# Attention by blocks of 512 queries, with a block's output product, norm and FFN issued between the next block's scores and the FFN weight parts kept in DRAM

## The chip, the core and the metric

One NeuronCore of one Trainium2 chip runs the whole program. The metric is the device time of one execution in microseconds (us). A core has a matrix engine (PE, with its own weight loads, PEld), a vector engine (DVE), a scalar engine (ACT), a general engine (POOL) and a queue engine (SP) that here issues most DMAs. Each engine takes its instructions in the order in which they were put down; engines wait for one another by semaphores.

## The reference, cut to what matters

One transformer block on 2048 rows of 576 numbers in f32, with 32 heads of 18 numbers each and a hidden width of 4608:

```
x = A_x                                            # 1 x 2048 x 576
h = x + softmax(q k^T / sqrt(18)) v @ wo           # q, k, v = layernorm(x) @ wqkv, 32 heads
g, u = layernorm(h) @ w_gate, layernorm(h) @ w_up  # 576 x 4608 each
out = h + (gelu_tanh(g) * u) @ w_down              # 4608 x 576
```

## The kernel before

**Numbers.** Every large product is made of f16 pieces: a matrix is kept as a high part and a low part, and `products` lists the 14 pairs of 128-row pieces that `accumulate` multiplies into one PSUM bank (three pairs for each of four full row chunks, two for the 64-row rest). A chunk of 512 output columns is thus 14 matmuls 512 wide, a half row block (288 columns) 14 matmuls 288 wide. The down product uses 12 matmuls 288 wide per chunk (four hidden tiles, three pairs).

**Stages.** First the rows are normed, split and transposed by DMA into `X`, and q, k (`qk_tile`) and v (`v_rows`) are made; q and k go to DRAM as `qk_hi` and `qk_lo`, v stays in SBUF. Then come 32 attention stages: eight groups of four heads (outer loop), and for each group four blocks of 512 queries (inner loop). A stage has 16 key tiles with two head pairs each: 32 slots. A slot has

- two score matmuls of one head pair (`scores_pair`, line 461; each uses 56 rows of the array, the two lie in different halves) into one of two PSUM pairs, and one ACT exponential over both (line 463), 128 x 1024 numbers;
- two matmuls (line 420) and two DVE maxima (line 423) of a stage that lies 56 slots ahead (`maxima`), through three PSUM banks `bank0` to `bank2`; the maxima become two rows of the next stages' q operand (`max_finish`);
- in every second slot the four f32 matmuls of `weigh` (line 467) that multiply the exponentials with v; each fills 32 of the 128 partitions of `acc`, and the trace shows each as two.

After a stage `out_block` transposes, divides and stores its result in f16 parts. Remaining q, k and v products run in between at the start (`other_products`). With the last group, `wo_block` of a finished query block fills in. When all attention is done the FFN runs: for 9 chunks of 512 hidden columns and 4 row blocks, `gate_up` makes 4 x 2 chunks of 14 matmuls, and `down` of the chunk before 8 chunks of 12. The FFN weights of a chunk are loaded from the inputs once, and split on ACT and DVE beside the chunk before.

**Order.** Inside `tc.manual_schedule` the PE order is the order of the code; the other engines' order is set by the framework's scheduler. The FFN lies behind that region.

Of the kernel before, what the change touches and what calls it, by code (L numbers as in the profile page):

```python
# [8 lines left out]

F16 = mybir.dt.float16  # L10
# [6 lines left out]
P = 128  # L17
# [8 lines left out]
MSC = 4096.0  # L26


@with_exitstack
def tile_block(  # L30
# [16 lines left out]

    nc = tc.nc
# [5 lines left out]
    TB = min(512, S)  # L54
    NB = S // TB
    TPB = TB // P
    FT = 4
    FC = FT * P
    NCH = DF // FC
    QK = 2 * D  # L60
    NG = H // 4
    R1 = 3 * DH

# [6 lines left out]
    pairs2 = [ps.tile([P, 2, 512], F32, name=f"pair{i}") for i in range(2)]  # L70
    singles = [ps.tile([P, 512], F32, name=f"bank{i}") for i in range(4)]
# [5 lines left out]
    pair_ring = ring(pairs2)  # L77
    single_ring = ring([p[:, i] for i in range(2) for p in pairs2])
    m_ring = ring(singles[:3])
    down_ring = ring(singles)  # L80


    nat = const.tile([P, NT, D], F32, name="nat")
    V = const.tile([P, 9936], F32, name="V")
    X = const.tile([P, 18432], F16, name="X")
    W = const.tile([P, 18048], F16, name="W")
    WK = const.tile([P, 2 * (NK + 1) * D], F32, name="WK")
    A = const.tile([P, 3 * 2048], F32, name="A")
# [25 lines left out]
    def exponents(views, name):  # L114

        n = len(views)
        k = views[0].shape[1]
        ac = small.tile([P, n, k], F32, tag=f"ac{n}", name=f"ac_{name}")
        am = small.tile([P, n], F32, tag=f"am{n}", name=f"am_{name}")
        for i, v in enumerate(views):  # L120
            for c in range(k):
                nc.vector.tensor_reduce(ac[:, i, c : c + 1], v[:, c], axis=AX.X, op=ALU.max,
                                        apply_absolute_value=True)
                yield
        nc.vector.tensor_reduce(am, ac, axis=AX.X, op=ALU.max)
        yield
        pt = next(m_ring)
        for i in range(n):
            nc.tensor.transpose(pt[0:1, i * P : (i + 1) * P], am[:, i : i + 1], id32)
        a1 = small.tile([1, n], F32, tag=f"a1{n}", name=f"a1_{name}")  # L130
        nc.vector.tensor_reduce(a1, pt[0:1, : n * P].rearrange("o (n p) -> o n p", n=n),
                                axis=AX.X, op=ALU.max)
        nc.vector.tensor_scalar_max(a1, a1, 2.0 ** -60)
        yield
        pb = next(m_ring)
        nc.tensor.matmul(pb[:, :n], ones[0:1], a1, start=True, stop=True)
        ab = small.tile([P, n], F32, tag=f"ab{n}", name=f"ab_{name}")
        nc.vector.tensor_copy(ab, pb[:, :n])
        e = small.tile([P, n], I32, tag=f"e_{name}", name=f"e_{name}")
        nc.vector.tensor_scalar(e, ab.bitcast(I32), 23, None, op0=ALU.logical_shift_right)  # L140
        yield
        return e

    def norm_exponent(v, name):

        q = small.tile([P, 2], F32, tag="nq", name=f"nq_{name}")
        j = view(A, 8 * 2 * 2 * D, (NK, D), F16)
        nc.scalar.activation(j, v[:, :NK], AF.Square, accum_out=q[:, 0:1])
        nc.scalar.activation(j[:, 0], v[:, NK], AF.Square, accum_out=q[:, 1:2])
        pb = next(m_ring)  # L150
        nc.tensor.matmul(pb[:, :2], ones, q, start=True, stop=True)
        a = small.tile([P, 1], F32, tag="na", name=f"na_{name}")
        nc.vector.tensor_reduce(a, pb[:, :2], axis=AX.X, op=ALU.add)
        nc.vector.tensor_scalar_max(a, a, 2.0 ** -110)
        e = small.tile([P, 1], I32, tag=f"e_{name}", name=f"e_{name}")
# [605 lines left out]
```

## Time and profile before

| | |
|---|---|
| median of three runs | 3018.15 us (3017.2 to 3020.59) |
| the profiled execution | 3017.52 us, of which its span (first to last instruction) is 3015.8 us |
| mean granted PE clock | 0.995 |
| DVE, ACT, POOL busy | 1993.3, 1454.6 and 62.9 us |
| DMA | 95.14 MB moved, mean 32 GB/s |
| first maxima, first scores, end of attention | about 95, 223 and 1693 us after the span's start |

Busy time of PE is modelled from matmuls that overlap; how much work PE really has is read from the start of one matmul to the start of the next. A line number in a row is that of the source line; many matmuls carry the line of the helper `accumulate` (267), so that the tiles' names tell them apart.

### The profile page before, as it was taken

The page shows a single profiled execution, that of the slowest core. Times are in us where ns is not written, and L with a number is a line of the kernel's source. Part 1 is how long each engine was busy: PE and PEld are TensorE (multiplying, and loading weights), DVE is VectorE, ACT ScalarE, POOL GpSimd, SP SyncE. Part 2 cuts the span into 40 slices and gives each one's busy share as a digit, 9 for nine tenths or more (in the row PEclk, how much of TensorE's full clock was granted, in tenths as well). Part 3 has the DMA queues.
Part 4 walks back from the last instruction along what each step waited for, and adds up shares of the span by engine and source line. Part 5 has one row for each costly group of instructions (what it writes and reads, how often), then busy time and mean ns, then how long its engine had stood idle before and what let it go on. Part 6 is the DMA issues. An engine that isn't in the chain of part 4 may idle for free.

```text
span 3015.8 us, 42951 instructions
## 1 busy us (share of the span) xinstructions
PE 2792.8 (93%) x17312; PEld 1154.9 (38%) x17312; DVE 1993.3 (66%) x3711; ACT 1454.6 (48%) x1716; POOL 62.9 (2%) x137
## 2 busy tenths in 40 slices
PE   6998888888888888888889999999999999999999
PEld 3531112212111211211123455555555555555555
DVE  7569999999999999999996653443435252524222
ACT  5227777777777777777757422121212121212111
POOL 0000000000000000000000000000000000000000
PEclk9999999999999999999999999999999999999999
DMA  8121000000100000000023420110101010100001
GB/s 222 49 87 32 1 25 1 25 1 1 25 1 25 1 24 2 1 24 5 29 48 87 100 67 7 45 33 19 51 1 52 1 51 1 51 1 1 1 16 48
DMA packets 105433, 95.14 MB, mean 32 GB/s; under 512 B 65872, under 2 KB 79312, under 8 KB 105232
## 3 DMA queue, kind: packets, MB, share of 16 engines
q1 hardware_dynamic: 100256, 83.81, 9.8%
q0 software_dynamic: 4976, 8.56, 1.1%
q8 instruction: 136, 2.23, 0.3%
q14 instruction: 65, 0.53, 0.1%
HBM read 63.70 MB, written 14.16 MB: 26 GB/s over the span
## 4 chain that ended last, share of the span: by engine, by line
PE 74%; DVE 18%; ACT 4%; issue 2%; DMA 2%; SPq 0%; DVEq 0%; ACTq 0%
PE pair L267 30%; PE bank L267 16%; DVE mx L423 15%; PE bank L467 14%; PE bank L420 9%; PE pair L461 4%; ACT WK L463 1%; ACT W L238 1%; ACT V L238 1%; PE bank L480 1%; DVE o L485 0%; ACT V L598 0%; DVE nat L491 0%; DMA A<-qk_hi 0%; DMA WK<-in_A_wqkv_dram 0%
## 5 line engine op out<-in xcount | busy, mean ns | idle before, releaser
L423 DVE TENSOR_REDUCE mx<-bank 128x1 f32<-128x512 f32 x2048 | 1283.2, 682 | 138.4 <-PE bank L420 137.4
L463 ACT ACTIVATE WK<-pair,p_ex_sc 128x1024 f32<-128x1024 f32 x1024 | 1088.0, 1112 | 335.1 <-PE pair L461 333.4
L467 PE MATMUL bank<-WK,V 128*32 128x512 f32 x4096 | 551.9, 610 | 0.1
L267 PE MATMUL pair<-X,V 128*128 128x512 f16 x2240 | 489.0, 379 | 3.1 <-ACT ga L613 3.1
L267 PE MATMUL pair<-X,W 128*128 128x512 f16 x2128 | 469.0, 379 | 1.5 <-ACT ga L613 1.5
L615 DVE SCALAR_TENSOR_TENSOR ga<-pair,p_hsc,ga 128x512 f32<-128x512 f32 x144 | 107.7, 748 | 502.4 <-PE pair L267 502.4
L420 PE MATMUL bank<-W 54*128 54x512 f16 x1024 | 291.5, 378 | 93.2 <-DVE mx L423 91.1
L267 PEld LDWEIGHTS <-WK 128*128 128x128 f16 x3456 | 338.2, 98 | 93.2
L420 PE MATMUL bank<-A 54*128 54x512 f16 x1024 | 283.0, 380 | 80.5 <-DVE mx L423 77.7
L613 ACT ACTIVATE ga<-pair,p_gsc 128x512 f32<-128x512 f32 x144 | 98.8, 686 | 490.2 <-PE pair L267 490.2
L267 PEld LDWEIGHTS <-W 128*128 128x128 f16 x2296 | 222.2, 98 | 273.1 <-issue 16.9
L267 PEld LDWEIGHTS <-V 128*128 128x128 f16 x2240 | 218.7, 98 | 261.6 <-issue 3.9
L616 ACT CAST WK<-ga 128x512 f16<-128x512 f32 x144 | 88.9, 618 | 442.9 <-DVE ga L615 442.9
L634 DVE SCALAR_TENSOR_TENSOR nat<-bank,p_dsc,nat 128x288 f32<-128x288 f32 x288 | 147.9, 515 | 194.9 <-PE bank L267 194.9
L467 PEld LDWEIGHTS bank<-WK,V 128*32 128x32 f32 x4096 | 81.3, 108 | 504.5 <-issue 469.0
L267 PE MATMUL bank<-V,WK 128*128 128x288 f16 x1920 | 239.0, 286 | 0.0
L461 PE MATMUL pair<-W 56*128 56x512 f16 x1024 | 199.1, 384 | 5.8 <-ACT WK L463 5.6
L461 PE MATMUL pair<-A 56*128 56x512 f16 x1024 | 199.9, 385 | 0.3 <-DVE qk L322 0.2
L267 PE MATMUL bank<-W,WK 128*128 128x288 f16 x1536 | 191.4, 286 | 0.0
L617 DVE TENSOR_TENSOR WK<-ga,WK 128x512 f16<-128x512 f32 x144 | 99.3, 690 | 76.3 <-ACT WK L616 76.1
L461 PEld LDWEIGHTS <-W 56*128 56x128 f16 x1024 | 50.2, 94 | 247.9 <-issue 221.0
L461 PEld LDWEIGHTS <-A 56*128 56x128 f16 x1024 | 50.5, 95 | 241.3 <-issue 211.0
(154 smaller groups left out, 1122.0 us busy)
## 6 DMA issues: line engine op xcount, KB each, us to landing
V<-in_B_w_down_dram SPq DMA_DIRECT2D x9, 1152.0 KB
A<-in_B_w_gate_dram SPq DMA_DIRECT2D x9, 1024.0 KB
A<-in_B_w_up_dram SPq DMA_DIRECT2D x9, 1024.0 KB
qk_hi<-qk SPq DMA_DIRECT2D x36, 128.0 KB
qk_lo<-qk SPq DMA_DIRECT2D x36, 128.0 KB
A<-in_A_x_dram SPq DMA_DIRECT2D x32, 144.0 KB
out_dram<-nat SPq DMA_DIRECT2D x16, 288.0 KB
WK<-in_A_wqkv_dram SPq DMA_DIRECT2D x3, 1152.0 KB
```

What stands on the lines that cost most here:

```text
L238: nc.scalar.activation(wh[:, c], wf[:, c], AF.Copy, scale=sc)
L267: nc.tensor.matmul(dst, a, b, start=(i == 0), stop=(i == len(pairs) - 1))
L420: nc.tensor.matmul(pms[j][:, :TB], Q[r, q0 : q0 + P], K[r, kc * TB : (kc + 1) * TB], start=True, stop=True)
L423: nc.vector.tensor_reduce(mx[:, t, 2 * pr + j, kc : kc + 1], pms[j][:, :TB], axis=AX.X, op=ALU.max)
L461: nc.tensor.matmul(pS[:, j, :TB], K[r, kt * P : (kt + 1) * P], Q[r, qc * TB : (qc + 1) * TB], start=True, stop=True)
L463: nc.scalar.activation(pes[(2 * kt + pr) % NPE], pS[:, :, :TB], AF.Exp, scale=ex_sc)
L467: nc.tensor.matmul(acc[32 * hh : 32 * hh + 32, :TB], Vg[n // NB][:, kt * G4 + hh * VC : kt * G4 + hh * VC + 32], pes[(2 * kt + hh // 2) % ...
L613: nc.scalar.activation(ga, pg[:, :TB], AF.Gelu_apprx_tanh, scale=gsc)
L615: nc.vector.scalar_tensor_tensor(ga, pu[:, :TB], hsc, ga, op0=ALU.mult, op1=ALU.mult)
L616: nc.scalar.copy(hh[:, f], ga)
L617: nc.vector.tensor_sub(hl[:, f], ga, hh[:, f])
L634: nc.vector.scalar_tensor_tensor(nat[:, t, ws], pt[:, :HALF], dsc, nat[:, t, ws], op0=ALU.mult, op1=ALU.add)
```

## The change

**Order of the work.** The query block becomes the outer loop: four blocks of 512 queries, each with eight head groups, still 32 stages of 32 slots. When a block's eight groups are done, its output product, norm and FFN (`wo_block`, `ffn`, `down`, now generators that give up control after each matmul with its price in us) are put in a queue (`Filler`). The stages of the next block take from it: `fill.spend` three times per key tile, about 4 matmuls at a time. The last block's FFN runs alone at the end. In block 0 the queue holds the remaining q, k and v products.

**Memory.** Each stage loads its K (all keys), Q (512 queries) and V from DRAM into one of three sets; v is written to DRAM first (`v_d`). The FFN now goes over its 36 hidden tiles once for each row block; in the first pass a tile's weights are loaded from the inputs, split on ACT and POOL (`prepare`) and written to DRAM (`gu_d`, `dn_d`), later passes load the parts back. The scales of the split come from sums of squares over all FFN weights (`norms`, 54 loads and ACT squares, issued in block 0).

**PSUM.** The scores have one pair of banks `sc` (before: two); the maxima keep three banks; `fb` are two banks for everything from the queue; `acc` holds the weighted sums.

**FFN arithmetic.** gelu is made of Square and Tanh on ACT and two DVE operations, in place of one table function.

```diff
-    pairs2 = [ps.tile([P, 2, 512], F32, name=f"pair{i}") for i in range(2)]
-    singles = [ps.tile([P, 512], F32, name=f"bank{i}") for i in range(4)]
+    sc = ps.tile([P, 2, 512], F32, name="sc")
+    mb = [ps.tile([P, 512], F32, name=f"mb{i}") for i in range(3)]
+    acc = ps.tile([P, 512], F32, name="acc")
+    fb = [ps.tile([P, 512], F32, name=f"fb{i}") for i in range(2)]
...
+    def spend(self, us):
+        self.budget += us
+        while self.budget > 0:
+            if not self.step():
+                self.budget = 0.0
...
-    def accumulate(dst, pairs):
+    def accumulate(dst, pairs, cost):
         for i, (a, b) in enumerate(pairs):
-            if i == len(pairs) // 2:
-                yield
             nc.tensor.matmul(dst, a, b, start=(i == 0), stop=(i == len(pairs) - 1))
+            if i < len(pairs) - 1:
+                yield cost
...
+    def norms():
+        for i in range(NH):
+            fs = slice(2 * i * P, 2 * (i + 1) * P)
+            for k, w in enumerate((w_gate, w_up, w_down)):
...
+                nc.scalar.activation(s, s, AF.Square, accum_out=q_w[:, k, i : i + 1])
+                yield
...
+    def prepare(q):
...
+        if q >= NF:
+            nc.sync.dma_start(gu.rearrange("p a c n -> p (a c n)"), gu_d[f])
+            nc.sync.dma_start(dn.rearrange("p a n -> p (a n)"), dn_d[f])
+            return
...
+            nc.scalar.activation(hi, w, AF.Copy, scale=s)
+            nc.gpsimd.tensor_scalar(w, w, s, None, op0=ALU.mult)
+            nc.gpsimd.tensor_sub(lo, w, hi)
...
+    def ffn(b):
...
+                nc.scalar.activation(h, pg[:, :TB], AF.Square, scale=g_sq[:, G : G + 1])
+                nc.vector.scalar_tensor_tensor(h, h, 1.0, pg[:, :TB], op0=ALU.add, op1=ALU.mult)
+                nc.scalar.activation(h, h, AF.Tanh, scale=g_th[:, G : G + 1])
+                nc.vector.scalar_tensor_tensor(h, h, 1.0, pg[:, :TB], op0=ALU.add, op1=ALU.mult)
+                prepare(q + 2)
...
+                nc.vector.scalar_tensor_tensor(h, pu[:, :TB], 2.0 ** -46, h,
+                                               op0=ALU.mult, op1=ALU.mult)
+                nc.scalar.copy(ht[:, 0], h)
+                nc.gpsimd.tensor_sub(ht[:, 1], h, ht[:, 0])
...
+            if b == 0:
+                rate = 0.33
+            else:
+                rate = (ffn_us - (LEFT if b == 1 else 0.0)) / (NG * SLOTS)
             for kt in range(NT):
-                for pr in range(2):
-                    scores_pair(n, kt, pr)
-                    take(mxs, UPS // NT)
-                    if g < NG - 1 or kt >= NT // 4:
-                        take(fill)
-                    take(side)
-                if prev is not None:
-                    weigh(*prev)
+                for p in range(2):
+                    scores_pair(n, kt, p)
+                    if p == 0:
+                        if prev is not None:
+                            weigh(*prev)
...
+                        take(mxs)
+                        fill.spend(rate * 0.7)
+                    else:
+                        fill.spend(rate * 0.6)
+                        take(mxs)
+                        fill.spend(rate * 0.7)
...
+                if b > 0 and g == 0 and kt == 5:
+                    fill.push(f"wo{b - 1}", wo_block(b - 1))
+                    fill.push(f"ffn{b - 1}", ffn(b - 1))
```

**The PE order before**, in the middle of the attention stages: `pair` are the score banks, `bank0` to `bank2` those of the maxima, `bank3` the weighted sum, `W` the operands of q and k.

```order
L467 MATMUL bank3_71<-WK_76,V_73 32x512 x4
L461 LDWEIGHTS W_75
L461 MATMUL pair0_66<-W_75 128x512
L461 LDWEIGHTS W_75
L461 MATMUL pair0_66<-W_75 128x512
L420 LDWEIGHTS W_75
L420 MATMUL bank1_69<-W_75 128x512
L420 LDWEIGHTS W_75
L420 MATMUL bank2_70<-W_75 128x512
```

Scores and maxima follow one another until the next `weigh`; all of them use half the rows of the array, so that the way in which the array is divided changes twice in a key tile, to the 32-column matmuls of `weigh` and back.

**The PE order now**, at a place in the third query block, where the queue holds a `down` product: `sc` are the score banks, `mb` those of the maxima, `fb` those of the queue, `SET` the operands of a stage, `OV` those of the FFN.

```order
L465 MATMUL sc_66<-SET_73 128x512
L472 MATMUL acc_70<-PES_74,SET_73 32x512 x4
L429 LDWEIGHTS SET_73
L429 MATMUL mb2_69<-SET_73 128x512
L429 LDWEIGHTS SET_73
L429 MATMUL mb0_67<-SET_73 128x512
L263 LDWEIGHTS OV_77
L263 MATMUL fb0_71<-OV_77 128x288
L263 LDWEIGHTS OV_77
L263 MATMUL fb0_71<-OV_77 128x288
```

Seven such FFN matmuls stand here, then scores, seven more, maxima, eight more, a transpose of `out_block` and the next scores. They use the whole array, so that its division changes eight times in a key tile. Counted over the whole program, two neighbouring matmuls differ in this 1311 times before and 3851 times now, at the same number of matmuls of each shape in attention and the large products: 770, 993, 1029 and 968 times in the four query blocks.

**The ACT order now**, in the second query block: line 467 is the exponential, 659 the Square and 661 the Tanh of one hidden tile, 671 its f16 copy, 638 a weight part, 493 a cast of an attention result.

```order
L659 ACTIVATE h_9565<-fb1_72,g_sq_368 128x512
L467 ACTIVATE PES_74<-sc_66,p_ex_sc_359 128x1024
L661 ACTIVATE h_9565<-h_9565,g_th_369 128x512
L467 ACTIVATE PES_74<-sc_66,p_ex_sc_359 128x1024
L638 ACTIVATE OV_77<-OV_77,s_w_367 128x640
L467 ACTIVATE PES_74<-sc_66,p_ex_sc_359 128x1024
L671 CAST OV_77<-h_9565 128x512
```

Before, the exponentials stood here one after the other, with nothing else between them for most of a stage; now the scheduler has put the FFN's operations singly between them.

More of the change, by code (lines that the diff above doesn't have):

```diff
@@ L1 @@
 import math
+from collections import deque
 from contextlib import ExitStack
@@ L111, in tile_block, with exponent_of @@
     nc.gpsimd.memset(neg, -MSC)
[L114 to L123, printed above, removed]
-                yield
[L125 to L153, printed above, removed]
+    def exponent_of(a, name, pool=small):
         nc.vector.tensor_scalar_max(a, a, 2.0 ** -110)
-        e = small.tile([P, 1], I32, tag=f"e_{name}", name=f"e_{name}")
+        e = pool.tile(list(a.shape), I32, tag=f"e_{name}", name=f"e_{name}")
         nc.vector.tensor_scalar(e, a.bitcast(I32), 23, None, op0=ALU.logical_shift_right)
@@ L269, in run, with split_cols @@
[L269 to L282 removed]
+    def split_cols(wf, s, wh, wl):
+        nc.scalar.activation(wh, wf, AF.Copy, scale=s)
+        nc.vector.scalar_tensor_tensor(wl, wf, s, wh, op0=ALU.mult, op1=ALU.subtract)
     qk_hi = dram.tile([QK, S], F16, name="qk_hi")
```

682 lines of the change are left out of this document (359 added, 323 removed).

## The prediction

> **What bounds the kernel now.** I read the page first, then the windows of five stages, then PE's timeline in one stretch of each kind.
>
> ```profile
> PE 2792.8 (93%) x17312; PEld 1154.9 (38%) x17312; DVE 1993.3 (66%) x3711; ACT 1454.6 (48%) x1716; POOL 62.9 (2%) x137
> 0.00:95.30 95.30, 66.40 (x384) 38.54 (x385) 57.71 (x173) 44.06 (x107) 10.23 (x32) 1.00 0.79 205
> 95.30:222.80 127.50, 126.04 (x690) 57.27 (x691) 86.09 (x137) 24.65 (x96) 1.91 (x4) 1.00 0.15 50
> 222.80:1693.00 1470.20, 1288.39 (x8609) 312.24 (x8605) 1321.18 (x2372) 1123.31 (x1107) 43.52 (x88) 0.99 0.09 22
> 1722.00:3015.80 1293.80, 1283.09 (x7453) 729.07 (x7451) 509.00 (x980) 257.35 (x399) 7.27 (x14) 1.00 0.08 27
> 1839.88 24.17 PE pair L267 x112
> 1864.05 11.76 PE bank L267 x96
> 88.44 8.58 DMA A<-qk_hi
> ```
>
> A window row has its length, then busy us of PE, PEld, DVE, ACT and POOL, the granted clock, the DMA share and GB/s. The last three rows come from the chain of waits (the load of q and k there is used below): one FFN chunk of one row block is 24.17 + 11.76 us of matmuls without a gap. So a 512-wide matmul takes 24.17/112 = 0.2158 us, a 288-wide one 11.76/96 = 0.1225 us, and 36 such pieces give 1293.5 us: the FFN's own window. That half is bound by PE and can't shrink; it can only be put where PE is idle. Such room is in attention (1470 us), and how much of it is seen in one key tile:
>
> ```profile
> 702.48 0.39 PE L461 MATMUL pair<-A 56*128 56x512 f16 x2
> 702.70 0.38 PE L420 MATMUL bank<-W 54*128 54x512 f16 x2
> 702.92 0.38 PE L461 MATMUL pair<-A 56*128 56x512 f16 x2
> 703.14 0.38 PE L420 MATMUL bank<-W 54*128 54x512 f16 x1
> 703.86 0.37 PE L420 MATMUL bank<-W 54*128 54x512 f16 x1 [0.35 <-DVE mx L423]
> 704.17 1.07 PE L467 MATMUL bank<-WK,V 128*32 128x512 f32 x8
> 705.16 0.39 PE L461 MATMUL pair<-A 56*128 56x512 f16 x2
> 703.12 2.48 DVE L423 TENSOR_REDUCE mx<-bank 128x1 f32<-128x512 f32 x4 [0.20 <-PE bank L420]
> 702.97 2.12 ACT L463 ACTIVATE WK<-pair,p_ex_sc 128x1024 f32<-128x1024 f32 x2 [0.57 <-PE pair L461]
> L423 DVE TENSOR_REDUCE mx<-bank 128x1 f32<-128x512 f32 x2048 | 1283.2, 682 | 138.4 <-PE bank L420 137.4
> ```
>
> Starts are 2.68 us apart (702.48 to 705.16): DVE works 2.48 of them, and PE waits for a bank that DVE frees. PE's work is 0.22 for each of four pairs and 0.99 for `weigh` with the change behind it; 703.86 to 704.17 is a pair (0.22) and a change of 0.09. Together 1.96 us, so 0.72 us of this tile are free. On average a tile takes 1470.2/512 = 2.87: (2.87 - 1.96) x 512 = 466 us, less some 70 of output products and transposes that stand there too, about 395 us. That is all that the change can win.
>
> **The price of mixing.** The change pays in a coin that the trace shows in its first stage, where q and k products lie between maxima:
>
> ```profile
> 143.05 0.39 PE L420 MATMUL bank<-A 54*128 54x512 f16 x2
> 143.38 1.68 PE L267 MATMUL pair<-X,W 128*128 128x512 f16 x7
> 144.99 0.39 PE L420 MATMUL bank<-A 54*128 54x512 f16 x2
> 97.46 1.89 PE L267 MATMUL pair<-W,X 128*128 128x288 f16 x14
> 99.28 0.39 PE L420 MATMUL bank<-A 54*128 54x512 f16 x2
> 99.60 0.67 PE L267 MATMUL pair<-W,X 128*128 128x288 f16 x4
> ```
>
> A pair of maxima that takes 0.22 among its like takes 0.33 and 0.32 here, seven wide matmuls take 1.61 in place of 7 x 0.2158 = 1.51, and fourteen narrow ones 1.82 in place of 1.715. Each time the division of the array changes (whole, halves, 32 columns), 0.10 to 0.11 us are lost, with PE waiting for no engine. I take 0.105. The order shows 3851 changes in place of 1311: 2540 x 0.105 = **267 us more** of PE time, if all of it lies where PE is the bound.
>
> The Trainium skill, page "TensorEngine Tiling (Array Packing)", section Key Properties, says that changing the tiling mode drains the engine; the rows above agree, and put 0.105 us on it. Its page "TensorE: Matmul & The Clock Gate", Part 2, says that weight loads are pulled ahead of running matmuls; by that alone a change would be free, and the sum would be the first rival's. The rows speak for the drain.
>
> **The new sum, stage by stage** (us of PE unless said).
>
> *Up to the first scores.* The matmuls ahead of the first maxima differ by 14 narrow ones (1.7 us). The 24 loads of a set now all stand on SP, where POOL had half; at 0.6 us each (below), part of them behind the last store, I take 100 for 95. Then 42 steps of maxima in place of 56, with 21 wide and 224 narrow matmuls between: 4.5 + 27.4 + 42 x 0.22 + 84 x 0.105 = 50; DVE 42 x 1.24 = 52. With `max_finish` 55. V now comes back from DRAM before the first `weigh`: 5 us, between nothing and 9 (the 8.58 us that a first q load took on the chain). **160.**
>
> *Block 0.* The scores have one pair of banks, so scores wait for the exponential before.
>
> ```profile
> L463 ACT ACTIVATE WK<-pair,p_ex_sc 128x1024 f32<-128x1024 f32 x1024 | 1088.0, 1112 | 335.1 <-PE pair L461 333.4
> L245 ACT ACTIVATE W<-WK,p_s_w 128x1920 f16<-128x1920 f32 x2 | 3.8, 1880 | 0.0
> L245 ACT ACTIVATE W<-WK,p_s_w 128x640 f16<-128x640 f32 x1 | 0.8, 827 | 1.3 <-DVE p_s_w L166 1.3
> ```
>
> From scores to the exponential's start is 702.97 - 702.48 = 0.49, it lasts 1.11, and PE is back 0.06 later (the first maximum, 703.12 + 0.68, ends at 703.80, PE goes on at 703.86): 1.66 us per slot at least. The slot with `weigh` has 0.22 + 0.89 + 0.22 + 0.22 and four changes, 1.97; the other is held at 1.66. A tile takes 3.63, without fillers 3.32: 6 stages of 16 x 3.63 and 2 of 16 x 3.32 = 455. The 42 squares of 1152 or 1280 numbers that the order shows between this block's exponentials take 1.25 to 1.35 each (the two L245 rows give 0.823 ns per number); where they delay an exponential, about 0.65: 27. Fill products that must be done at once (`require`) 10, output blocks and ACT evictions 13. **505**; before, eight stages took about 367 (128 x 2.87).
>
> *Blocks 1 to 3.* Block 2 has 1008 wide (217.5) and 976 narrow matmuls (119.6), 128 tiles of 4 x 0.22 + 0.89 (226.6), 1029 changes (108), and transposes:
>
> ```profile
> L480 PE MATMUL bank<-id,WK 128*128 128x128 f32 x128 | 21.0, 286 | 0.0
> L438 PE MATMUL bank<-id,mm 128*32 128x128 f16 x32 | 7.3, 229 | 0.8 <-DVE mm L433 0.8
> ```
>
> 8 x (21.0 + 7.3)/32 = 7. Sum 679, or 5.3 us per key tile. Block 1 (892 wide, 784 narrow, 993 changes) 626, block 3 (as block 2, with 84 maxima fewer and 968 changes) 663: **1968**. Here PE is the bound, since ACT and DVE per tile need less:
>
> ```profile
> L613 ACT ACTIVATE ga<-pair,p_gsc 128x512 f32<-128x512 f32 x144 | 98.8, 686 | 490.2 <-PE pair L267 490.2
> L616 ACT CAST WK<-ga 128x512 f16<-128x512 f32 x144 | 88.9, 618 | 442.9 <-DVE ga L615 442.9
> L615 DVE SCALAR_TENSOR_TENSOR ga<-pair,p_hsc,ga 128x512 f32<-128x512 f32 x144 | 107.7, 748 | 502.4 <-PE pair L267 502.4
> L634 DVE SCALAR_TENSOR_TENSOR nat<-bank,p_dsc,nat 128x288 f32<-128x288 f32 x288 | 147.9, 515 | 194.9 <-PE bank L267 194.9
> ```
>
> ACT: 2 x 1.11 and 36/128 of a hidden tile (2 x 0.69 + 0.62 = 2.0) = 2.8; in block 1 also three weight parts (0.83, 0.83, 0.76), 3.5. DVE: 2.48, 36/128 x 3 x 0.75 and 72/128 x 0.52 = 3.4. So cover is there on average, but not at each place: Square, Tanh and two DVE operations run after one another before a queue bank is free, with exponentials and maxima queued behind each of them in order, and the next scores waiting for those exponentials. A slot leaves 2.65 - 1.66 = 1.0 us of slack. I allow 0.4 us per hidden tile (108: 43), 0.7 us more for each of 36 weight splits in block 1 (25), and 22 where the FFN waits for the transposed norm (its chain below): **90**, between 0 and 2.5 us per hidden tile (270), as a Square, a wait and a Tanh (0.69 + 0.75 + 0.69) with all of their cover gone give.
>
> POOL's multiply and subtract have no row. The nearest are its memsets and DVE's subtract:
>
> ```profile
> L251 POOL MEMSET V<- 64x512 f16 x10 | 5.2, 519 | 951.8 <-PE pair L267 674.3 <-PE bank L467 141.3 <-ACT WK L463 136.1
> L251 POOL MEMSET W<- 64x1728 f16 x1 | 1.5, 1532 | 0.1
> L617 DVE TENSOR_TENSOR WK<-ga,WK 128x512 f16<-128x512 f32 x144 | 99.3, 690 | 76.3 <-ACT WK L616 76.1
> 695.89 4.28 SPq L446 DMA_DIRECT2D A<-mT  x7
> ```
>
> Between 0.52 and 1.53 us; I take 1.0, nearer DVE's 0.69: seven per hidden tile are 7 us, beside 626/36 = 17 us of PE. Covered, at no cost; it would cost only above 2.5 us each. SP issues a DMA every 0.6 us (4.28/7): per stage 33 and in block 1 another 41, 44 of 78 us. What stands behind a waiting DMA on SP are the rows of maxima, needed ten slots (26 us) later. The reloaded parts are 0.95 MB per hidden tile; at the 205 GB/s of the first window 4.6 us, under the 9 us that a tile takes even in the tail. All this I cost at nothing.
>
> *Tail.* Behind the last `weigh` the order has 1124 wide and 1168 narrow matmuls: 242.6 + 143.1 = 386. What before lay between attention and FFN, a wait for norm and transpose,
>
> ```profile
> 1693.15 13.91 PE bank L267 x112
> 1707.08 0.53 DVE nat L547
> 1714.29 3.20 DMA X<-V
> ```
>
> 10.4 us from the last output product to the first transposed rows (1707.08 to 1717.49), is covered for the most part by `down` products left over; 10. The last store 4. **400.**
>
> Sum: 160 + 505 + 1968 + 90 + 400 = 3123. Against the profiled execution: 3123 of span and the 1.7 us that lie around it before (3017.5 - 3015.8) make **3125 us**. The median of the runs is 0.6 above that execution, which changes nothing.
>
> **Rivals.** *Changes are free.* If the weights of the next kind are loaded while the last matmul runs, 267 us go: 2858, and the kernel is faster. The point where it turns: 3125 - 3017 = 108 us over 2540 changes, so a change must cost under 0.105 - 0.043 = 0.062. Against it: five places above, all at 0.09 to 0.11, with PE dense. 0.08. *No stalls and all of block 0's extras hidden.* The 90, and the 27 and 10, go: 2998. For it: the scheduler has put one exponential between Square and Tanh everywhere. Against it: before, key tiles cost 2.87 on average with two score pairs, when DVE needed 2.48. 0.07. *The chain of ACT and DVE decides.* One score pair and two queue banks make each hidden tile lose 2.5 us: 3125 - 90 + 270 = 3305. For it: the single buffers. Against: the slack of 1.0 us. 0.14. *Weight preparation is late in block 1.* POOL at 3 us per operation, 21 us per hidden tile for 17: 4 x 36 = 144, 3269; or SP holds up the loads. No row shows POOL reading a tensor. 0.08. The order leaves no doubt that the change does what it says.
>
> **Chances and range.** Forecast 0.63 (3050 to 3220). Measurement can tell 0.2%, 6 us. Faster: 0.08, 0.05 of the second rival, and 0.02 of the forecast's low end, 0.15; within 0.2%: 0.03; slower 0.82. The range takes in the second rival's upper part and the late weights: 3000 to 3270; outside are free changes, and most of the third rival.
>
> **What would show it.** Key tiles of 5.3 us in block 2 with PE pitches of 0.33 for a pair between queue matmuls; 3.3 to 3.6 in block 0, PE waiting for exponentials of its one pair; a tail of 400 us. A pair at 0.22 between queue matmuls kills the price of mixing; idle PE with waits for ACT and DVE in blocks 1 to 3 beyond 90 us is the third rival, waits for POOL or a DMA the fourth.

## The result and the profile after

The changed kernel takes 3186.99 us (median of four runs, 3182.74 to 3192.03); the kernel before, beside it, 3017.68. The ratio is 1.056, with a 95% interval of 1.0541 to 1.0578: **slower by 169 us**. The forecast was 3125, 108 more than before.

Set against the terms of the prediction, from the starts of the first score matmuls of each stage in the trace, the tail from the start of the last `weigh` matmul (us; the profiled execution spans 3183.9):

| part | predicted | measured | off by |
|---|---|---|---|
| up to the first scores | 160 | 166.9 | +7 |
| block 0 | 505 | 542.7 | +38 |
| blocks 1 to 3, stalls included | 1968 + 90 | 2041.0 | -17 |
| tail | 400 | 433.3 | +33 |

The page of the changed kernel: busy time, the clock that PE was granted in 40 slices, and two of the costliest groups (as before: count, busy, mean ns, idle time ahead and what ended it).

```profile
span 3183.9 us, 45415 instructions
PE 2949.0 (93%) x17250; PEld 1089.6 (34%) x17250; DVE 1932.7 (61%) x3551; ACT 1645.3 (52%) x1865; POOL 512.6 (16%) x387
...
PEclk9988999989999999999999999998999999989999
...
L432 DVE TENSOR_REDUCE mx<-mb 128x1 f32<-128x512 f32 x2048 | 1320.6, 685 | 718.3 <-PE mb L429 713.3
...
L465 PE MATMUL sc<-SET 56*128 56x512 f16 x2048 | 409.8, 394 | 107.5 <-ACT PES L467 103.5
```

PE is busy for 93% of the span, as before; the share says nothing of what went wrong. The maxima tell more: DVE now waits 713 us for PE at line 432 where before it waited 137 (row of line 423 in the prediction), so PE has become the engine that the rest waits for. Its busy time grew from 2792.8 to 2949.0 us with 62 matmuls fewer. That goes with the mixing (the version in bursts below, which hardly mixes, has 2797.3), though this modelled time shows less than the price found below. PE itself waits 103.5 us for exponentials, of the one score pair.

The windows of the stretches (length, then busy us of PE, PEld, DVE, ACT, POOL, the granted clock, DMA share, GB/s): the first and the last stage of block 0, block 1, and a steady stretch of block 2.

```profile
166.90:249.10 82.20, 63.78 (x300) 14.91 (x300) 42.90 (x71) 55.87 (x65) 0.00 (x0) 0.78 0.55 162
632.20:709.60 77.40, 51.59 (x264) 10.77 (x264) 44.18 (x89) 45.25 (x47) 40.35 (x26) 0.80 0.36 116
709.60:1372.00 662.40, 632.22 (x3766) 210.01 (x3765) 444.51 (x805) 412.29 (x463) 328.03 (x215) 0.99 0.37 113
1644.80:2051.00 406.20, 406.16 (x2446) 142.32 (x2446) 267.67 (x454) 213.16 (x229) 25.48 (x22) 1.00 0.24 76
```

In the steady stretch PE has next to no gap (0.04 of 406.20 us). Elsewhere it has gaps, and where they are long the granted clock falls too: 0.78 in the first stage, 0.80 in the last of block 0. The 32 stages one after another (us, from the starts of their first scores, the last one to the start of the last `weigh`):

```
block 0   82.1  73.8  67.2  68.1  59.7  58.8  55.6  77.4
block 1   79.2  80.8  82.1  83.2  87.2  83.2  82.8  84.0
block 2   85.0 102.9  84.9  85.0  85.2  85.1  84.9  84.9
block 3   85.1 101.1  84.9  85.0  85.2  85.1  81.1  73.2
before    44.4 in nearly every stage
```

PE's timeline in block 2 (start, us from the first start to the modelled last end, instruction, count), to be read by the starts:

```profile
1602.54 0.39 PE L465 MATMUL sc<-SET 56*128 56x512 f16 x2
1602.86 1.07 PE L472 MATMUL acc<-PES,SET 128*32 128x512 f32 x8
1603.86 0.39 PE L429 MATMUL mb<-SET 54*128 54x512 f16 x2
1604.18 1.03 PE L263 MATMUL fb<-OV 128*128 128x288 f16 x7
1605.15 0.39 PE L465 MATMUL sc<-SET 56*128 56x512 f16 x2
1605.47 1.03 PE L263 MATMUL fb<-OV 128*128 128x288 f16 x7
1606.43 0.39 PE L429 MATMUL mb<-SET 54*128 54x512 f16 x2
1606.76 1.19 PE L263 MATMUL fb<-OV 128*128 128x288 f16 x6
1607.88 0.39 PE L465 MATMUL sc<-SET 56*128 56x512 f16 x2
```

From 1602.54 to 1607.88 is one key tile, 5.34 us with no wait shown. A pair of scores takes 0.32, `weigh` 1.00, a pair of maxima 0.32, seven narrow matmuls 0.97 where 7 x 0.1225 is 0.86: each of the eight changes of the array's division shows its 0.1 us. The stage's 84.9 us are 5.31 per tile; 5.3 was predicted. In block 0 the same view:

```profile
561.90 0.39 PE L465 MATMUL sc<-SET 56*128 56x512 f16 x2 [0.30 <-ACT PES L467]
562.22 1.07 PE L472 MATMUL acc<-PES,SET 128*32 128x512 f32 x8
563.22 0.39 PE L429 MATMUL mb<-SET 54*128 54x512 f16 x2
563.54 0.39 PE L263 MATMUL fb<-OV 128*128 128x512 f16 x1
563.87 0.39 PE L465 MATMUL sc<-SET 56*128 56x512 f16 x2
564.19 0.39 PE L263 MATMUL fb<-OV 128*128 128x512 f16 x1
564.51 0.39 PE L429 MATMUL mb<-SET 54*128 54x512 f16 x2
564.83 0.39 PE L263 MATMUL fb<-OV 128*128 128x512 f16 x1
565.52 0.39 PE L465 MATMUL sc<-SET 56*128 56x512 f16 x2 [0.30 <-ACT PES L467]
```

561.90 to 565.52 is 3.62 us (predicted 3.63), with 0.30 of PE waiting for the exponential. So both unit prices held; the misses lie in places that are no steady tile. The handover from one query block's FFN to the next block's output product, on three engines' rows in order of time (SPq is SP's queue issuing a DMA):

```profile
1483.64 0.42 SPq L695 DMA_DIRECT2D out_dram<-ACC  x1
...
1488.53 0.34 SPq L587 DMA_DIRECT2D ACC<-in_A_x_dram  x1
...
1491.39 0.94 DVE L593 SCALAR_TENSOR_TENSOR ACC<-fb,u_o,ACC 128x288 f32<-128x288 f32 x2 [7.63 <-DMA ACC<-in_A_x_dram]
...
1491.96 1.60 PE L263 MATMUL fb<-OV 128*128 128x288 f16 x6 [9.17 <-DVE ACC L593]
...
1494.03 1.93 PE L472 MATMUL acc<-PES,SET 128*32 128x512 f32 x8
```

The output product needs its rows of x in an accumulator `accs[t % 5]`. That one still holds rows of the block before, which are stored at 1483.64; only then, at 1488.53, is the load of x issued. PE stands for 9.17 us, and after that runs at half speed for a while: from 1491.90 to 1496.00 us the granted clock is 0.50, and `weigh` takes 1.93 us where it takes 1.07 in a steady tile. This is the stage of 102.9 us, and block 3's of 101.1. The first section of the Trainium skill's page "TensorE: Matmul & The Clock Gate" (Part 1) says that PE falls to half its clock after at least one idle window of some 3.4 us; the granted clock and the two `weigh` rows agree. The last stage of block 0, the first weight parts on ACT and PE's wait behind them:

```profile
676.44 0.83 ACT L638 ACTIVATE OV<-OV,s_w 128x640 f16<-128x640 f32 x1 [7.13 <-DMA OV<-in_B_w_gate_dram]
...
678.32 0.61 PE L465 MATMUL sc<-SET 56*128 56x512 f16 x2 [7.25 <-ACT PES L467]
```

ACT stands before a copy whose weights have not come, an exponential stands behind that copy in ACT's order, and the next scores need the exponential: PE waits 7.25 us for "an exponential", and the reason is a DMA. Not all of this stage's waits are of that kind: at 652.43 six copies of weight parts in a row, which wait for no load, take 4.30 us of ACT, and PE then waits 3.49 us for an exponential.

### The profile page after: what moved, and what is told of

It is laid out like the page before. It is cut to its first block, busy times and chain, and to the rows that moved or that the text cites. A ratio compares the mean times of both kernels' runs of the same rounds, so it can differ in the third digit from the quotient of the medians.

```text
span 3183.9 us, 45415 instructions
## 1 busy us (share of the span) xinstructions
PE 2949.0 (93%) x17250; PEld 1089.6 (34%) x17250; DVE 1932.7 (61%) x3551; ACT 1645.3 (52%) x1865; POOL 512.6 (16%) x387
## 4 chain that ended last, share of the span: by engine, by line
PE 76%; DMA 6%; ACT 6%; issue 5%; DVE 4%; POOL 2%; SPq 1%; ACTq 0%; POOLq 0%; DVEq 0%
PE fb L263 36%; PE acc L472 13%; PE sc L465 9%; PE mb L429 8%; PE mb L263 5%; ACT PES L467 4%; PE sc L263 3%; DMA OV<-in_B_w_down_dram 2%; POOL OV L639 2%; PE acc L263 1%; DVE mx L432 1%; ACT OV L549 1%; POOL OV L640 1%; DMA ACC<-in_A_x_dram 1%; DMA OV<-in_B_w_gate_dram 1%
## 5 line engine op out<-in xcount | busy, mean ns | idle before, releaser
L432 DVE TENSOR_REDUCE mx<-mb 128x1 f32<-128x512 f32 x2048 | 1320.6, 685 | 718.3 <-PE mb L429 713.3
L467 ACT ACTIVATE PES<-sc,p_ex_sc 128x1024 f32<-128x1024 f32 x1024 | 1138.5, 1112 | 922.5 <-PE sc L465 915.4
L263 PE MATMUL fb<-OV 128*128 128x512 f16 (+1 forms) x6476 | 1380.4, 342 | 42.8 <-DVE ACC L593 23.5
L263 PEld LDWEIGHTS <-OV 128*128 128x128 f16 x8888 | 779.5, 98 | 853.8 <-issue 421.8
L472 PE MATMUL acc<-PES,SET 128*32 128x512 f32 x4096 | 564.3, 624 | 3.5 <-DMA SET<-v_d 3.5
L465 PE MATMUL sc<-SET 56*128 56x512 f16 x2048 | 409.8, 394 | 107.5 <-ACT PES L467 103.5
L429 PE MATMUL mb<-SET 54*128 54x512 f16 x2048 | 433.6, 395 | 18.8 <-DVE mx L432 11.1
L672 POOL TENSOR_TENSOR OV<-h,OV 128x512 f16<-128x512 f32 x144 | 166.5, 1157 | 1682.0 <-ACT OV L671 1682.0
L639 POOL TENSOR_SCALAR OV<-OV,s_w 128x640 f32<-128x640 f32 (+1 forms) x108 | 197.5, 1829 | 818.2 <-ACT OV L638 753.0
L263 PE MATMUL mb<-OV 128*128 128x512 f16 (+1 forms) x982 | 172.3, 335 | 0.9 <-DMA OV<-ACC 0.9
L263 PE MATMUL sc<-OV 128*128 128x512 f16 (+1 forms) x656 | 125.5, 344 | 33.1 <-DVE ACC L593 12.4
L660 DVE SCALAR_TENSOR_TENSOR h<-h,fb 128x512 f32<-128x512 f32 x114 | 77.9, 684 | 110.3 <-ACT h L659 109.8
```

Source lines behind the costliest of these rows:

```text
L263: nc.tensor.matmul(dst, a, b, start=(i == 0), stop=(i == len(pairs) - 1))
L429: nc.tensor.matmul(pms[j][:, :TB], Q[r, t * P : (t + 1) * P], K[r, kc * TB : (kc + 1) * TB], start=True, stop=True)
L432: nc.vector.tensor_reduce(mx[:, t, 2 * p + j, kc : kc + 1], pms[j][:, :TB], axis=AX.X, op=ALU.max)
L465: nc.tensor.matmul(sc[:, j, :TB], K[r, kt * P : (kt + 1) * P], Q[r, :], start=True, stop=True)
L467: nc.scalar.activation(pes[(2 * kt + p) % NPE], sc[:, :, :TB], AF.Exp, scale=ex_sc)
L472: nc.tensor.matmul(acc[32 * hh : 32 * hh + 32, :TB], Vs[n % 3][:, c : c + 32], pes[(2 * kt + hh // 2) % NPE][:, hh % 2], start=(kt == 0), ...
```

## The experiments

All were timed in three rounds beside the kernel before; ratios are to it, with 95% intervals. The first group tests the terms of the sum, the second looks for a version that beats both kernels. A short list of what each gave, by the parts of the profile (us):

| run | median | first scores | block 0 | blocks 1-3 | tail |
|---|---|---|---|---|---|
| changed kernel | 3186.99 | 166.9 | 542.7 | 2041.0 | 433.3 |
| five changes per tile | 3102.08 | 168.2 | 539.8 | 1961.2 | 432.8 |
| ten changes per tile | 3244.95 | 166.1 | 543.5 | 2101.1 | 434.2 |
| no sums of squares | 3139.83 | 162.6 | 503.9 | 2035.8 | 433.5 |
| eight accumulators | 3141.41 | 166.1 | 546.8 | 2004.3 | 422.2 |
| half exponentials in block 0 | 3125.96 | 168.0 | 480.3 | 2042.2 | 433.1 |
| queue used in bursts | 3555.63 | 166.8 | 544.4 | 2426.3 | 419.3 |
| first and fourth together | 3050.71 | 166.6 | 533.7 | 1921.8 | 422.4 |
| own banks in block 0 | 3139.06 | 229.4 | 425.8 | 2045.8 | 432.9 |
| all combined | 2958.99 | 231.2 | 403.2 | 1924.6 | 405.6 |

**The price of mixing, from both sides.** Five changes of division per key tile in place of eight: the maxima stand right behind the scores, which use the array in the same halves.

```diff
                     scores_pair(n, kt, p)
+                    take(mxs)
                     if p == 0:
...
-                        take(mxs)
                         fill.spend(rate * 0.7)
                     else:
-                        fill.spend(rate * 0.6)
-                        take(mxs)
-                        fill.spend(rate * 0.7)
+                        fill.spend(rate * 1.3)
```

> Same instructions as the changed kernel, other PE order: maxima directly behind the scores of each slot, weigh behind them, the queue's matmuls once per slot. The array's division changes 5 times per key tile in place of 8. Theory (each change costs 0.1 us of PE, and blocks 1 to 3 are bound by PE): 3 x 384 tiles x 0.1 = 115 us less there, a stage of block 2 falls from 85.0 to about 80; block 0 perhaps 10 less; 3060 to 3075 us in all. Rival (the chain of exponential, Square, Tanh and the two queue banks sets the pace, PE's changes lie in time that would be waited anyway): within 20 us of 3187, PE's waits for ACT and DVE grow by what the changes give back.

And ten: the queue is also used on both sides of `weigh`.

```diff
                     if p == 0:
+                        fill.spend(rate * 0.23)
                         if prev is not None:
...
+                        fill.spend(rate * 0.23)
                         take(mxs)
-                        fill.spend(rate * 0.7)
+                        fill.spend(rate * 0.24)
```

> Same instructions, the queue's share of the first slot of a key tile cut in three (ahead of weigh, behind it, behind the maxima): 10 changes per key tile in blocks 1 to 3 in place of 8. Theory: 2 x 384 x 0.1 = 77 us more, 3264 us, a stage of block 2 at 88.2. Rival (ACT/DVE chain sets the pace): within 20 us of 3187.

Measured 1.0281 (1.0266 to 1.0296) and 1.0756 (1.074 to 1.0772). The same matmuls make stages of 80.2, 85.0 and 88.4 us in block 2: (85.0 - 80.2)/(16 x 3) = 0.100 us and (88.4 - 85.0)/(16 x 2) = 0.106 us per change. The prediction took 0.105. PE's timeline of the first of the two kernels, same block:

```profile
1602.50 0.39 PE L465 MATMUL sc<-SET 56*128 56x512 f16 x2
1602.73 0.38 PE L429 MATMUL mb<-SET 54*128 54x512 f16 x2
1603.04 1.07 PE L472 MATMUL acc<-PES,SET 128*32 128x512 f32 x8
1604.04 1.25 PE L263 MATMUL fb<-OV 128*128 128x512 f16 x5
```

The score pair, followed by its like, is back at 0.23 us. That free changes would make the kernel faster (the first rival) is refuted: they are not free. The whole gain, 85 us, was less than the 112 to 127 expected: block 0, where the exponential's chain decides, gained 3 (it moves by as much with an edit that does not touch it: 546.8 with eight accumulators); block 1 fell from 662 to 648 only, with two stages at 89.7 and 85.5, and PE's waits for exponentials grew there from 18.8 to 34.6 us; and the handover in block 3 gained nothing (101.7 for 101.1).

**The sums of squares.** This kernel leaves out the sums of squares over the FFN weights (54 loads and ACT squares) and puts constants in their place; the scales of the split come from those.

```diff
-        for i in range(NH):
...
+        nc.gpsimd.memset(q_w[:, :2], 0.355)
+        nc.gpsimd.memset(q_w[:, 2:], 0.04)
+        yield
```

> Leaves out the sums of squares over the FFN weights (54 rounds of loads, 54 squares on ACT in the first stages); their result is set to a constant. Theory: the squares stand between exponentials of a single score pair, so stages 0 to 3 of block 0 (82, 74, 67 and 68 us) fall to the 58 to 62 of stages 4 and 5: 40 to 50 us less, 3140 us. Rival (what is long in these stages is the half clock, the lumps of q and k products and the V load): 27 us less or fewer, stages 0 and 1 stay above 65.

1.0415 (1.0393 to 1.0436), 47 us below the changed kernel, as expected; block 0 fell by 39, all of it in its first four stages (70.8, 63.2, 60.3, 58.3). Those were expected at 58 to 62: the first stayed well above, so something else holds it too, which was not followed up. The last stage kept its 77.9: that one is not the squares' doing.

**The accumulators.** Eight in place of five, so that x can be loaded before the rows of the block before are stored.

```diff
-    ACC = const.tile([P, 5 * D], F32, name="ACC")
+    ACC = const.tile([P, 8 * D], F32, name="ACC")
...
-    accs = [view(ACC, 4 * D * i, (D,)) for i in range(5)]
+    accs = [view(ACC, 4 * D * i, (D,)) for i in range(8)]
 
     def acc_of(t):
-        return accs[t % 5]
+        return accs[t % 8]
```

> Eight row accumulators in place of five, so that the x rows of a block's output product need not wait until the block before has stored its rows. Theory (at the handover PE waits for the chain last down product, output store, x load, add): stages 17 and 25 fall from 102 to about 85 to 88, the tail loses 12 us of gaps: 40 to 50 us less, 3140 us. Rival (the wait there is for norm and transposed rows, which the accumulators don't change): 10 us less at most.

1.0413 (1.0396 to 1.0431). The two stages of 102.9 and 101.1 became 83.9 each, the tail fell by 11: 46 us for three tiles of memory. The waits in the changed kernel (us in total, times, longest) that the edit was to take away:

```profile
PE fb L263 <- DVE ACC L593: 23.5, 5, 9.2
DVE ACC L593 <- DMA ACC<-in_A_x_dram: 28.7, 9, 7.6
```

19 + 17 + 11 us went, somewhat more than the waits themselves: these 23.5, and 12.4 more that the page puts down to the same adds before matmuls into `sc`, in the tail. The slower clock behind such a wait fits the difference.

**What bounds block 0.** In this kernel block 0's exponentials cover half their columns, and constants stand for the other half.

```diff
-        nc.scalar.activation(pes[(2 * kt + p) % NPE], sc[:, :, :TB], AF.Exp, scale=ex_sc)
+        w = TB // 2 if n < NG else TB
+        nc.scalar.activation(pes[(2 * kt + p) % NPE][:, :, :w], sc[:, :, :w], AF.Exp, scale=ex_sc)
```

> In block 0 alone the exponential works on half of the columns (the other half of the weights is left at a constant), about 0.4 us less on ACT per slot; PE and DVE keep all their work. Theory (in block 0 the single score pair is the bound: scores, exponential, scores): the slot without weigh falls to what PE needs, 1.30 us, so a key tile of stages 4 and 5 from 3.6 to about 3.3 us, the stage from 59 to 52 or 53; block 0 from 543 to about 495, 3140 us in all. Rival (block 0 is bound by DVE's maxima or by PE): stages 4 and 5 stay within 1 us of 59.

1.0353 (1.0333 to 1.0372); block 0 took 480.3, less than expected, but not where it was expected. The exponential takes 0.68 us instead of 1.11. Stages 4 and 5 (counted from 0), expected at 52 or 53, took 60.6 and 55.3, where they had 59.7 and 58.8; 53 of the 62 us came from stages 0 to 3 and 7, where the squares and the weight parts share ACT. The scheduler had moved ACT's order: stage 4 now holds seven squares in place of two, and stage 5 five in place of none. Stage 6 has no squares and no weight parts in either kernel, so that it compares cleanly; it fell by 6.5, from 55.6 to 49.1. With the chain out of the way PE is next in line, as in a dense part of stage 4: its timeline has a key tile from 445.70 to 448.96, 3.26 us, without a wait, with three queue matmuls in it, each between two changes. So the chain of one score pair does set the tiles with nothing else on ACT, as stage 6 shows, but mixed PE work stands only 0.36 us per tile (5.8 per stage) behind it.

**Is there a price-free way to mix?** Blocks 1 to 3 without queue work inside a stage, and a stage's share in one piece at its end.

```diff
-                rate = (ffn_us - (LEFT if b == 1 else 0.0)) / (NG * SLOTS)
+                rate = 0.0
...
+            if b > 0:
+                fill.spend((ffn_us - (LEFT if b == 1 else 0.0)) / NG)
```

> In blocks 1 to 3 the queue isn't used between the scores of a stage; a stage's share of it is issued in one piece at the stage's end. Changes of the array's division fall from 8 to 2 per key tile. Theory (mixing costs 6 changes but hides the FFN in the exponential's wait, since with one score pair a key tile takes 3.3 us for 2 us of PE): a stage of block 2 takes 16 x 3.32 + 337/8 = 95 us in place of 85; about 240 more, 3420 us. Rival (the mixing is what made the kernel slow; without it the FFN costs its plain time): 230 us less than now, 2960 us.

1.1784 (1.1766 to 1.1802), longer than either theory expected. Without queue matmuls between, nothing covers PE's wait for its one score pair:

```profile
L465 PE MATMUL sc<-SET 56*128 56x512 f16 x2048 | 423.5, 402 | 278.7 <-ACT PES L467 274.1 <-DMA SET<-mT 3.8
```

274.1 us against 103.5. Stages of block 2 took 96.5 in place of 85.0, so with this PSUM plan the mixing, dear as it is, saves 11 us a stage against doing the work apart. Block 1 was longer still (94 to 109 per stage); why was not resolved.

**A second score pair for block 0, wrong and right.** In block 0 the queue needs its two banks `fb` for q, k and v products only. If those are done ahead of the first scores, the banks can hold every second score pair. The first form made the two banks halves of one tile:

```diff
-    fb = [ps.tile([P, 512], F32, name=f"fb{i}") for i in range(2)]
+    fbp = ps.tile([P, 2, 512], F32, name="fbp")
+    fb = [fbp[:, i] for i in range(2)]
...
+        pS = fbp if n < NG and p else sc
...
-            fill.spend(0.75)
-            if i % 4 == 0:
+            fill.spend(2.45)
+            if i % 2 == 0:
                 take(nrm)
-        fill.require("v3")
+        fill.all()
...
-                        if (2 * kt + p) % 5 == 0:
+                        if (2 * kt + p) % 7 == 0:
```

> In block 0 the two banks of the queue serve as a second score pair; the q, k and v products that lay between block 0's scores are all issued ahead of them, between the first maxima. Theory (the one pair bounds block 0, at 1.66 us per slot): stages of block 0 fall from 58 to 82 us to the 44 to 48 of the kernel before, apart from the last with its first weight parts; 160 us less there, 70 more ahead of the first scores: 90 less, 3097 us. Rival (sums of squares, loads and maxima hold block 0): stages stay at 58 or more, and the kernel is up to 70 us slower than the changed one.

It missed by far: 4121.18 us, 1.3652 (1.3629 to 1.3675). The queue's matmuls in its profile, and the same group in the changed kernel:

```profile
L264 PE MATMUL fbp<-OV 128*128 128x512 f16 (+1 forms) x6476 | 1517.2, 363 | 739.2 <-DVE h L664 365.5 <-DVE ACC L693 192.6 <-DVE h L670 107.1
```

```profile
L263 PE MATMUL fb<-OV 128*128 128x512 f16 (+1 forms) x6476 | 1380.4, 342 | 42.8 <-DVE ACC L593 23.5
```

PE's idle time ahead of them rose from 42.8 to 739.2 us. Half of it (365.5 us) is ended by line 664, DVE's last read of the gate product in one half, ahead of the up product that goes to the other half: the order of accesses is kept per tile, and two halves of one tile are no double buffer. The same flaw stood in a combination with five changes and eight accumulators, run beside it:

> The two pairs in block 0, eight accumulators and the order with 5 changes per key tile together. Theory (the three causes lie in different stretches and add up): 3187 - 90 - 46 - 85 = 2966 us, under the kernel before. Rival (one bound stands behind them all, and what one gives the next can't give again): above 3040 us.

3882.28 us, 1.2864 (1.2844 to 1.2883): a miss for the same reason. With two separate banks, each with an exponential of its own over 512 columns (and the first form's edits to the queue and the squares):

```diff
+        second = n < NG and p == 1
         for j in range(2):
             r = half(j, R1 + 2)
-            nc.tensor.matmul(sc[:, j, :TB], K[r, kt * P : (kt + 1) * P], Q[r, :],
+            nc.tensor.matmul(fb[j] if second else sc[:, j, :TB], K[r, kt * P : (kt + 1) * P], Q[r, :],
                              start=True, stop=True)
+        if second:
+            for j in range(2):
+                nc.scalar.activation(pes[(2 * kt + p) % NPE][:, j], fb[j], AF.Exp, scale=ex_sc)
+            return
```

> As e8 for block 0 (q, k and v products ahead of the first scores, a second place for scores), but the queue's two banks stay two tiles: every second slot's scores go to them, with one exponential of 512 columns for each. e8 made the two banks halves of one tile. Theory (there the queue's products then waited for the other half's readers in blocks 1 to 3; the one pair bounds block 0): blocks 1 to 3 are back at 85 us per stage, stages 0 to 6 of block 0 take 46 to 50 us, first scores 70 us later; 3187 - 145 + 70 = 3110 us. Rival (sums of squares, loads and maxima hold block 0): stages at 58 or more, 3190 us or more.

1.0402 (1.0386 to 1.0417). Blocks 1 to 3 are back at 2046, which shows that the tile's halves had been the flaw. Block 0 takes 425.8 instead of 542.7, of which 62.5 are paid back ahead of the first scores; 48 us remain between the medians, where 77 had been expected: the first seven stages took 50.1 to 58.9 us and not 46 to 50. Why was not followed up.

**Adding up.** Five changes and eight accumulators in one kernel:

> e1 and e4 together. Theory (changes in every key tile, accumulators at two handovers and in the tail: different stretches): 3187 - 85 - 46 = 3056 us. Rival (part of what e1 gave back was the wait at the handovers): 3075 us or more.

1.0111 (1.0096 to 1.0126): 136 us below the changed kernel where the two alone gave 85 and 46. With the separate banks of block 0, and in the tail a ring of single banks without the two halves of `sc`:

```diff
-        rings["f"] = ring([*fb, *mb, sc[:, 0], sc[:, 1], acc])
+        rings["f"] = ring([*fb, *mb, acc])
```

> f1, eight accumulators, 5 changes per key tile, and in the tail a ring of six single banks without the two halves of the score tile. Theory (the causes lie in different stretches and add up): 3110 - 85 - 46 - 15 = 2965 us, under the kernel before. Rival (one bound behind them all): above 3040 us.

2958.99 us (2955.82 to 2966.58), ratio **0.9803 (0.9787 to 0.9819)**: this version beats the kernel before by 2.0% (1.8 to 2.1%), as expected. Its tail is 405.6 where five changes and eight accumulators alone have 422.4: two PSUM banks fewer make it 17 us shorter. In that longer tail PE waits 16.5 us for DVE ahead of matmuls into `sc`:

```profile
PE sc L263 <- DVE h L668: 8.1, 10, 0.8
PE sc L263 <- DVE ACC L691: 6.1, 10, 0.6
PE sc L263 <- DVE ACC L593: 2.3, 2, 1.2
```

Without the two halves these waits are gone. That the halves had waited for one another's readers, as those of `fbp` did, fits this, but no run separates it from the rest of the ring's order.

Block 1 then still lost most to ACT (PE waited 35.9 us for exponentials there), so POOL was given ACT's share of the weight split:

```diff
-            nc.scalar.activation(hi, w, AF.Copy, scale=s)
+            nc.gpsimd.tensor_scalar(hi, w, s, None, op0=ALU.mult)
```

> f2 with the high weight parts of the first pass made on POOL in place of ACT. Theory (in block 1 and at the end of block 0 exponentials stand behind ACT copies that wait for a weight load): block 1 falls from 662 us by 20 to 35 beyond what f2 gives, the last stage of block 0 from 77 to 55; 40 us less than f2. Rival (POOL, with 3 x 1.9 us more per hidden tile, becomes late and holds the weight parts back): block 1 is longer than in f2.

2981.57, 0.9883 (0.9869 to 0.9898): 23 us longer than the kernel that it was to improve. POOL's timeline in block 1, and PE's waits there:

```profile
957.04 1.88 POOL L643 TENSOR_SCALAR OV<-OV,s_w 128x640 f16<-128x640 f32 x1
959.01 1.88 POOL L644 TENSOR_SCALAR OV<-OV,s_w 128x640 f32<-128x640 f32 x1
960.97 1.40 POOL L645 TENSOR_TENSOR OV<-OV 128x640 f16<-128x640 f32 x1
```

```profile
PE sc L466 <- DMA SET<-mT: 47.7, 9, 13.1
...
PE sc L466 <- ACT PES L472: 7.7, 7, 1.9
```

The waits for exponentials fell from 35.9 to 7.7 us, as meant. In their place stand 47.7 us for the rows of maxima, 13.1 of them just ahead of the block's first scores; the kernel without this edit shows none in block 1. The rows are loaded by SP's queue, and there the stores of the split parts (lines 646 and 647) stand before them. The first two rows are with the edit, the other four without it:

```profile
SPq L646 <- POOL OV L645: 157.8, 29, 10.0
SPq L647 <- POOL OV L645: 133.5, 28, 9.4
...
SPq L646 <- POOL OV L645: 88.8, 30, 7.1
SPq L647 <- POOL OV L645: 72.0, 27, 3.3
SPq L647 <- ACT OV L643: 49.5, 10, 14.9
...
SPq L646 <- ACT OV L643: 44.2, 11, 7.5
```

The stores now wait 291 us, all of it for POOL; without the edit they waited 161 for POOL and 94 for ACT. The total differs by little, so the place counts: at the end of block 0 SP issues such a store at 625.63, thirteen weight loads behind it and the rows of maxima only at 635.15, and PE's wait of 13.10 us ends at 637.63. With that wait the last stage of block 0 grew from 54.0 to 59.8 us. This is the prediction's fourth rival (weight preparation late, or SP holding up the loads), brought about by a POOL that is busy for 515 of block 1's 664 us.

## Why the prediction was right, and where its sizes were off

The sign, the mechanism and the range held; the forecast was 62 us low, 61 of it in the four differences of the first table (7 + 38 - 17 + 33).

- **The price of mixing: right.** 0.105 us per change, read from the first stage of the kernel before, against 0.100 and 0.106 by two experiments. The steady tile of blocks 2 and 3 came out at 5.31 for 5.3. The rival of free changes fell with it. The Trainium skill's page "TensorE: Matmul & The Clock Gate", Part 2, has weight loads pulled ahead of running matmuls; a change is not hidden by that here, since 48 of them cost a stage 4.8 us.
- **The exponential's chain in block 0: right**, 3.62 us per tile for 3.63; halving the exponential bears it out in stage 6, while elsewhere the squares moved with it.
- **Block 0's extras: mis-sized.** The squares were put at 27 us and cost 39, measured by leaving them out. And "Fill products ... output blocks and ACT evictions" left out the first weight parts: the last stage, booked at 16 x 3.32 = 53, took 77.4, as `prepare` puts copies, about half of which wait for DMA, ahead of exponentials on ACT. The rule that the prediction used for block 1 (what is queued behind a waiting instruction) was not applied to the stage in which that work begins. 12 + 24 is nearly the whole miss of 38. That `prepare`'s copies are the cause of all 24 was read from the timeline and not tested by itself; six of them waited for no load.
- **Stalls in blocks 1 to 3: the sum near (73 for 90), but by luck, since its parts were wrong.** 43 us were booked for hidden tiles; blocks 2 and 3 show next to none (406.16 of 406.20 us busy in block 2's steady stretch). 25 were booked for weight splits; block 1 lies 36 above its PE work of 626. And "22 where the FFN waits for the transposed norm" was 34 (17.9 and 16.1 above a steady stage's 85.0), with another cause: the transposed rows cost 7.7 us once, and the wait is for x in an accumulator that is stored too late. Eight accumulators removed it. The rival in which ACT and DVE decide every tile is refuted, since a slot's slack of 1.0 us did suffice. Its price did not follow from its terms: 0.69 + 0.75 + 0.69 is 2.13 us per hidden tile and not 2.5, so 230 us and not 270.
- **The tail: mis-sized.** The same accumulators cost 11 us of it, and the pair's halves in the ring of banks, by leaving them out, some 17. "10 ... is covered for the most part" counted neither. The remaining 5 are not explained.
- **Ahead of the first scores** 167 for 160; the first maxima came at 106.2 and not at 100.
- **POOL: wrong and without consequence.** The multiply took more than the upper bound of 1.53 us:

```profile
L639 POOL TENSOR_SCALAR OV<-OV,s_w 128x640 f32<-128x640 f32 x72 | 135.5, 1883 | 674.4 <-ACT OV L638 639.0 <-PE sc L465 16.6 <-DMA OV<-in_B_w_up_dram 7.8
L640 POOL TENSOR_TENSOR OV<-OV 128x640 f16<-128x640 f32 x72 | 101.0, 1404 | 5.4
```

A memset and a subtract of DVE said nothing of POOL's multiply. The point from which it would count (2.5 us each) was right in kind: one more multiply per part, in the last experiment, was too much.

So where did the room of some 395 us go? In blocks 1 to 3, 24 stages took 1097 us before, and three quarters of the 1331 us behind attention make 998 more; both together now take 2041, a gain of 54. The mixing and 73 us of stalls (36 in block 1, 34 at the two handovers, 3 elsewhere) ate most of what was there to win. Block 0 lost 177 (365.4 to 542.7), where one score pair, the squares and the first weights meet and nothing is hidden but the 56 us won ahead of the first scores; and the last quarter of the FFN with its handover takes 433 in place of 333. 54 - 177 + 56 - 101 = -168, the difference of the two spans.

## What to carry to other kernels

Before work of one kind is put between work of another, count the changes of the array's division and price one of them in a place of the old profile where both kinds already meet: with 0.1 us each, 2540 changes cost more than half of the idle time that they were to fill, and putting like next to like gave 85 us back at no cost. Then look at the places that are no steady loop (the first stage with a new kind of work, the handover from one block to the next, the tail), ask there which buffer a load must wait for and which instruction stands in front of a needed one: here these gave nearly all of the miss, and three more buffers gave 46 us. A "double buffer" made of two halves of one tile was one buffer here, at the price of 4121 us in place of 3139.

## What the runs showed of the hardware that was not expected

- A wait of PE costs more than its length: behind 9.17 us without work, `weigh` took 1.93 us in place of 1.07. Even a stage in which PE is busy for 63.78 of 82.20 us (the first of the windows above) was granted 0.78 of the clock.
- POOL's multiply of 128 x 640 numbers by one scale per partition (1883 ns) is dearer than its subtract of two tensors of that size (1404 ns).
